# A dilated convolution on one core: the 16-channel scratch laid out by channel, its first chunk transposed by TensorE, a smaller clear, and new queue orders

## The chip, the cores and the metric

The kernel runs on one core of a Trainium2 chip. Its engines are TensorE (PE, with its weight loads PEld), VectorE (DVE), ScalarE (ACT), GpSimd (POOL) and SyncE (SP), which here only issues DMAs. Each engine works through its own list of instructions in order. The metric is the device time of one execution in microseconds (us); lower is better.

## The reference

x has 2 sequences of 16000 steps of 144 channels, all in bf16. A causal convolution with 15 taps, two steps apart, gives 288 channels; half of them go through tanh, half through a sigmoid, the product is multiplied by w_o.

```python
B, T, D, K = (2, 16000, 144, 15)
def reference(x, w, w_o):
    dil = 2
    pad = (K - 1) * dil
    xp = jnp.pad(x, ((0, 0), (pad, 0), (0, 0)))
    h = jnp.einsum('btc,cd->btd', xp[:, pad:pad + T, :], w[0])
    for i in range(1, K):
        off = pad - i * dil
        h = h + jnp.einsum('btc,cd->btd', xp[:, off:off + T, :], w[i])
    f = h[..., :D].copy()
    g = h[..., D:].copy()
    z = jnp.tanh(f) * _sigmoid(g)
    return z @ w_o
```

## The kernel before

The 32000 steps are cut into 128 runs of 250, one for each partition, so that step t of all runs is one tile of 128 x 144. The 250 tiles make two single tiles and 31 octets of eight; the octets after the first (octet 0) are worked in 15 pairs, m = 0 to 14, with two units each (r = 0, 1), 30 units in all. A unit gives eight output tiles.

Of the 144 channels, 128 (called A) need a transposed tile (channels on partitions) for each step, kept in XA. The other 16 (called B) of eight taps are packed on 128 partitions, in XB. The convolution is done with fewer products than taps by a scheme of differences: V, DU and DD hold differences of XA tiles, GX, GU, GV and GD differences of these between octets, and WS, WC, WD, WV and WT sums of weights. DVE makes them; PE multiplies them into PSUM banks (PS), and parts shared by several tiles (UX, UC, UD, UE) are added by DVE and POOL in float32. UE lies in the memory of Xp. ACT takes sigmoid and tanh from PSUM to TG, DVE multiplies the halves into Z (the gate), a DMA transposes Z to ZT, PE multiplies by WOR (w_o laid out for blocks of 128 columns), ACT copies to OS, and SP stores.

How data get to XA and XB after the prologue (stages `load_xchunk`, `load_xa`, `compact_chunk`, `load_xb`, lines 650 to 719):

- A chunk is 16 tiles, two octets. `load_xchunk` loads it to Xr (two buffers).
- `load_xa(o)`: ACT or DVE copies the A channels of octet o to STA (two buffers), SP issues a DMA transpose to XA (lines 678 to 683).
- `compact_chunk(ci)`: the B channels of the chunk go to C16 as 4 groups of 6 rows: two tiles copied (DVE or ACT, line 864) and four differences (POOL, line 668). SP issues a DMA transpose from C16 to T16 (line 669) and a store of T16 to the scratch S16 in DRAM (line 670). In S16 the order is group, row, channel, then 128 partitions.
- `load_xb(o)`: SP shifts part of the previous octet's XB by 32 partitions (XB<-XB) and loads the rest from S16 (line 695). Each load brings one or two groups, 16 channels by 6 or 12 rows of 256 B. For octet 1 and octet 2 the loads are split further, because the halo comes from XBh.

The prologue (0 to some 25 us) loads x to Xp and the weights in five pieces; PE transposes Xp tiles for XA, and the B channels of the prologue go through XBc (in the memory of XS) to XBh with 12 more PE transposes (`b_halo`, line 628). Before these, POOL clears two rows of XBc (line 615) and copies 32 elements (line 622). POOL also clears all of Z (line 546) and WOR (line 547), and issues the 16 loads of w_o to WOR (line 1200). Two matmuls against the identity (line 1126) open banks 6 and 7.

The order of every engine's work is written out by hand: `_Graph` numbers operations as they are added, and TABLE gives for each engine the list of these numbers in the order of issue; `place` follows it. ON_ACT lists the copies (`free_copy`) that ACT makes instead of DVE. Waits between engines are worked out from what each operation reads and writes, so an operation waits only for its own inputs, buffers and banks, but everything behind it on its engine waits with it. The constants DMA_LAT, FIRST, SEM_LAT, MM and each operation's `dur` are a planner's estimates; they choose which PSUM banks are used, and the order in which an operation's waits stand, and no instruction's length.

Of the kernel before, what the change touches and what calls it, by code (L numbers as in the profile page):

```python
# [12 lines left out]
DMA_LAT = 2.8  # L13
DMA_RATE = 280e3
FIRST = (1.12, 1.1)
# [1360 lines left out]
```

## Time and profile before

| | us |
|---|---|
| median of 3 runs | 312.39 |
| lowest, highest | 311.79, 314.02 |
| the profiled execution | 311.91 |
| its span, first to last instruction | 310.2 |

The profiled execution is 0.48 us under the median. The page gives busy time by engine and a picture of the span in 40 slices, each digit the busy share in tenths (9 is 90% or more):

```profile
PE   8998779999999999999999999999999999999995
DVE  2999799999997999999999999989989897998755
ACT  2698578788888899899988988999889999888885
POOL 3495440444331333433234443213343331233330
DMA  7937789597999798895749999699757569431543
```

PE is full but for the slices from 23 to 47 us and the last one. In every timeline row the columns are start, length, engine, line, instruction, output and inputs, count, and in brackets how long the engine stood before it and what released it. In the rows of groups (`| busy, mean ns | idle`), busy time is in us and the mean of one in ns.

### The profile page before, as it was taken

What the parts mean: (1) busy time and instruction counts of PE and PEld (TensorE: products, weight loads), DVE (VectorE), ACT (ScalarE), POOL (GpSimd) and SP (SyncE); (2) the same over time, 40 slices, a digit from 0 to 9 for tenths busy, and PEclk for the clock granted to TensorE, in tenths of its full rate; (3) what the DMA queues carried; (4) which work ended last, traced back from release to release, by engine and by line L of the source; (5) the groups of instructions that cost most, each with busy time, mean ns of one, the idle gap of its engine ahead of it and who ended that gap; (6) DMA issues with size and microseconds to landing.
All of it is one profiled execution on the core that took longest, in us unless ns stands there. A gap on an engine that the chain in (4) does not pass through costs nothing.

```text
span 310.2 us, 7389 instructions
## 1 busy us (share of the span) xinstructions
PE 299.9 (97%) x2553; PEld 234.1 (75%) x2553; DVE 279.5 (90%) x607; ACT 264.0 (85%) x786; POOL 110.4 (36%) x105
## 2 busy tenths in 40 slices
PE   8998779999999999999999999999999999999995
PEld 7876556777767788787778777777878777777874
DVE  2999799999997999999999999989989897998755
ACT  2698578788888899899988988999889999888885
POOL 3495440444331333433234443213343331233330
PEclk9999999999999999999999999999999999999999
DMA  7937789597999798895749999699757569431543
GB/s 212 300 61 183 174 206 225 132 244 176 190 201 220 137 279 192 193 211 130 196 128 200 230 229 233 99 204 244 164 143 151 163 152 182 125 90 50 142 100 130
DMA packets 107631, 54.48 MB, mean 176 GB/s; under 512 B 95549, under 2 KB 98445, under 8 KB 107595
## 3 DMA queue, kind: packets, MB, share of 16 engines
q1 hardware_dynamic: 107049, 53.63, 76.5%
q0 software_dynamic: 512, 0.33, 0.5%
q8 instruction: 20, 0.33, 0.5%
q14 instruction: 16, 0.13, 0.1%
q10 hardware_dynamic: 34, 0.05, 0.1%
HBM read 15.93 MB, written 10.69 MB: 86 GB/s over the span
## 4 chain that ended last, share of the span: by engine, by line
PE 83%; DMA 8%; DVE 5%; issue 1%; SPq 1%; ACT 1%; DVEq 0%
PE PS L811 72%; PE PS L921 8%; DMA XA<-STA 4%; DMA ZT<-Z 2%; PE PS L564 1%; DMA XB<-s 1%; DVE PS L1065 1%; DVE Xp L991 1%; PE PS L592 1%; DVE V L723 1%; DVE STA L864 1%; DVE DD L723 0%; SPq L695 0%; SPq L669 0%; DVE Z L838 0%
## 5 line engine op out<-in xcount | busy, mean ns | idle before, releaser
L1001 POOL TENSOR_TENSOR UX<-UC,XS 128x576 f32<-128x576 f32 x60 | 83.7, 1413 | 177.2 <-ACT UC L450 117.3
L811 PE MATMUL PS<-WB,XB 128*128 128x288 bf16 x360 | 101.8, 286 | 0.0
L964 ACT ACTIVATE PS<-PS 128x288 f32<-128x288 f32 x213 | 81.9, 418 | 7.8 <-PE PS L811 6.4
L811 PE MATMUL PS<-WA,GD 128*128 128x288 bf16 x450 | 88.0, 286 | 0.4 <-DVE PS L1065 0.2
L450 ACT ACTIVATE TG<-PS 128x288 bf16<-128x288 f32 x180 | 65.1, 418 | 6.8 <-PE PS L811 5.7
L864 ACT ACTIVATE OS<-PS 128x432 bf16<-128x432 f32 (+1 forms) x93 | 42.8, 493 | 16.5 <-PE PS L921 15.6
L1065 DVE TENSOR_TENSOR PS<-PS,Xp 128x288 f32<-128x288 f32 x120 | 50.1, 460 | 3.1 <-ACT OS L864 1.0
L811 PEld LDWEIGHTS PS<-WA,GD 128*128 128x128 bf16 x450 | 40.6, 98 | 15.7 <-DVE PS L1065 2.3
L991 DVE TENSOR_TENSOR Xp<-PS,UD 128x576 f32<-128x576 f32 x60 | 43.2, 753 | 10.3 <-PE PS L811 6.9
L1065 DVE TENSOR_TENSOR PS<-PS,UX 128x288 f32<-128x288 f32 x120 | 50.1, 459 | 0.7 <-POOL UX L1001 0.3
L811 PE MATMUL PS<-WS,GU 128*128 128x288 bf16 x210 | 44.8, 286 | 1.8 <-DMA XB<-s 1.8
L921 PE MATMUL PS<-WOR,ZT 128*128 128x144 bf16 (+1 forms) x322 | 40.8, 253 | 1.1 <-DMA ZT<-Z 1.1
L811 PEld LDWEIGHTS PS<-WB,XB 128*128 128x128 bf16 x360 | 35.2, 98 | 8.7
L811 PE MATMUL PS<-WC,GV 128*128 128x288 bf16 x210 | 37.9, 286 | 0.0
L811 PE MATMUL PS<-WD,DD 128*128 128x288 bf16 x210 | 34.0, 286 | 0.0
L921 PEld LDWEIGHTS PS<-WOR,ZT 128*128 128x128 bf16 x322 | 27.5, 98 | 7.3 <-DMA ZT<-Z 1.4
L453 ACT ACTIVATE TG<-PS 128x144 bf16<-128x144 f32 x140 | 29.8, 301 | 2.5 <-PE PS L811 1.9
L838 DVE TENSOR_TENSOR Z<-TG 128x576 bf16<-128x576 bf16 (+1 forms) x63 | 27.7, 442 | 3.9 <-ACT TG L450 3.3
L811 PEld LDWEIGHTS PS<-WS,GU 128*128 128x128 bf16 x210 | 19.9, 98 | 7.5 <-DVE GD L800 2.1
L811 PE MATMUL PS<-WC,GX 128*128 128x288 bf16 x120 | 23.5, 286 | 1.8 <-DVE Xp L991 1.8
L723 DVE TENSOR_TENSOR V<-XA 128x1024 bf16<-128x1024 bf16 (+2 forms) x38 | 23.6, 623 | 1.1 <-DMA XA<-STA 0.9
L811 PE MATMUL PS<-WT,DU 128*128 128x288 bf16 x120 | 24.5, 286 | 0.1
(98 smaller groups left out, 435.8 us busy)
## 6 DMA issues: line engine op xcount, KB each, us to landing
Xr<-in_x_dram SPq DMA_DIRECT2D x15, 648.0 KB, 5.1
out_dram<-OS SPq DMA_DIRECT2D x30, 288.0 KB, 3.1
XB<-XB SPq DMA_DIRECT2D x29, 288.0 KB, 3.4
XB<-s SPq DMA_DIRECT2D x60, 48.0 KB, 3.0
s<-T SPq DMA_DIRECT2D x15, 96.0 KB, 3.5
WA<-in_w_dram SPq DMA_DIRECT2D x2, 288.0 KB, 4.5
ZT<-Z SPq DMA_TRANSPOSE x32, 3.5
Xp<-in_x_dram SPq DMA_DIRECT2D x2, 252.0 KB, 4.4
```

The source lines that it names most:

```text
L450: return e.activation(bass.AP(t[:].tensor, off + (0 if st > 0 else n), [[row, NP], [st, 2], [1, n]]), bass.AP(PS[:].tensor, lo * 512 + c0, ...
L453: ins = e.activation(bass.AP(t[:].tensor, off + i * n, [[row, NP], [1, n]]), bass.AP(PS[:].tensor, q.phys * 512 + c0, [[8 * 512, NP], [1, ...
L564: g.add("pe", [lambda t: t.matmul(PS[:, BANK_O * 512:BANK_O * 512 + 128], lhsT=HEAT[:], rhs=HEAT[:], start=True, stop=True)] * n, r=["HEAT ...
L723: return g.add("dve", lambda v: v.tensor_tensor(dst(), a(), b(), ALU.subtract), r=r, w=wk, dur=dur, prio=2, lock=True)
L811: return lambda t: t.matmul(bank(b), lhsT=lhs(), rhs=rhs(), start=start, stop=True, skip_group_check=True)
L838: g.add("dve", lambda v: v.tensor_tensor(dst(), TG[:, s, 1, 2 * k:2 * k + n, :], TG[:, s, 0, 2 * k:2 * k + n, :], ALU.mult), r=[("TG", s, ...
L864: return (lambda e: e.activation(dst(), src(), ACT.Copy)) if eng == "act" else (lambda e: e.tensor_copy(dst(), src()))
L921: return t.matmul(PS[:, c0:c0 + n * D], lhsT=ZT[:, zt, blk_, :], rhs=WOR[:, wi_:wi_ + n, :].rearrange("p a b -> p (a b)"), start=first, st ...
L964: g.add("act", lambda e: e.activation(bank(c), bank(b), ACT.Copy), r=[("bank", b)], w=[("bank", c)], dur=0.29, prio=prio)
L991: return v.tensor_tensor(ue(u % NU, q, 0, 2).rearrange("p (v n) -> p v n", v=2), src, UD[:, u % NUD, :, :], ALU.add)
L1001: op = g.add("pool", lambda p: p.tensor_tensor(UX[:, u % NU, h, :, :], UC[:, 0, :, :], bass.AP(XS[:].tensor, h * N2, [[2 * N2, NP], [0, 2] ...
L1065: g.add("dve", lambda e, dst=dst, src=src, ua=ua: e.tensor_tensor(bank(dst), bank(src), ua(), ALU.add), r=[("bank", src), ("UX", us, h) if ...
```

## The change

Five things are changed together.

1. C16 is laid out channel, group, row instead of group, row, channel. Its copy and its subtraction now write two or four neighbouring elements at a time and read Xr at a step of one tile (288 B). S16 follows: a channel's 24 rows of a chunk lie together, and a load of one or two groups takes one run of 6 or 12 rows for each channel (1.5 or 3 KB), or two runs where the two groups lie in different chunks.
2. For chunk 0 alone, the DMA transpose is replaced by three PE transposes into bank 7 and one ACT copy to T16. The two matmuls of line 1126 are added after it.
3. POOL clears only columns 720 to 863 of the one Z buffer that octet -1 uses.
4. TABLE and ON_ACT are new. There is one operation more, so numbers from 117 on are one higher. ON_ACT has 14 copies instead of 11 (10 of C16 and 4 of STA, before 8 and 3).
5. The planner's constants and a few `dur` are changed.

```diff
-DMA_LAT = 2.8
+DMA_LAT = 3.2
-FIRST = (1.12, 1.1)
+FIRST = (1.12, 1.5)
...
-        C16 = sb("C16", [NP, NX, 4, 6 * DB], BF16)
+        C16 = sb("C16", [NP, NX, DB, 4, 6], BF16)
...
-        g.add("pool", lambda p: p.memset(Z[:], 0.0), w=[("Z", i) for i in range(NZ)], dur=1.2)
+        g.add("pool", lambda p: p.memset(Z[:, -1 % NZ, 5 * D:6 * D], 0.0), w=[("Z", -1 % NZ)], dur=0.25)
...
             def xr(t, n=4):
-                return bass.AP(Xr[:].tensor, (s * XCH + t) * D + DA, [[NX * XCH * D, NP], [4 * D, 4], [D, n], [1, DB]])
-            cc = C16[:, s, :, :].rearrange("p a (t c) -> p a t c", c=DB)
+                return bass.AP(Xr[:].tensor, (s * XCH + t) * D + DA, [[NX * XCH * D, NP], [1, DB], [4 * D, 4], [D, n]])
+            cc = C16[:, s, :, :, :]
...
+            if ci:
+                g.add("sp", lambda e: e.dma_start_transpose(T16[:, s, :, :], C16[:, s, :, :, :].rearrange("p a b c -> p (a b c)")), r=[("C16", s, 0), ("C16", s, 1)], w=[("T16", s)], dur=1.3, dma="xb", nbytes=3 * 32768)
+            else:
+                tb = HB[7]
+                g.add("pe", [lambda t, i=i: t.transpose(PSb[:, tb.phys * 1024 + 128 * i:tb.phys * 1024 + 128 * i + 128],
+                                                        C16[:, s, :, :, :].rearrange("p a b c -> p (a b c)")[:, 128 * i:128 * i + 128], ID[:]) for i in range(3)],
+                      r=[("C16", s, 0), ("C16", s, 1), "ID"], w=[("bank", tb)], dur=0.23)
+                g.add("act", lambda e: e.activation(T16[:, s, :, :].rearrange("p a b -> p (a b)"), PSb[:, tb.phys * 1024:tb.phys * 1024 + 384], ACT.Copy),
+                      r=[("bank", tb)], w=[("T16", s)], dur=0.42)
...
             def s16(q, n):
-                return bass.AP(S16, q * 6 * DB * 128, [[128, DB], [DB * 128, 6 * n], [1, 128]])
+                c, b = q // 4, q % 4
+                if b + n <= 4:
+                    return bass.AP(S16, (c * 384 + 6 * b) * 128, [[24 * 128, DB], [1, GR * n]])
+                return bass.AP(S16, (c * 384 + 6 * b) * 128, [[24 * 128, DB], [(384 - 18) * 128, 2], [1, GR]])
```

The lists of TABLE are too long to show. Read with the renumbering undone, they say, for the stretch that is spoken of below:

- SP: the first 17 issues are the same. Then, before: DMA transpose of chunk 0, XA for octets 1 and 2, an XB copy, the S16 store of chunk 0, two XB copies and a third, the DMA transpose of chunk 1, six XB loads, ZT, the Xr load of chunk 2, the S16 store of chunk 1, XA for octets 3 and 4. After: XA for octet 1, the S16 store of chunk 0, XA for octet 2, the Xr load of chunk 2, two XB copies, the DMA transpose of chunk 1, eight XB issues (octet 1 is whole with the fifth, octet 2 with the eighth), ZT, the S16 store of chunk 1, XA for octets 3 and 4.
- POOL: before: the clears of XBc, the copy of 32 elements, two WOR issues, the clear of Z, the C16 subtraction. After: the clears of XBc, two WOR issues, the copy, three WOR issues, the C16 subtraction; the clear of Z stands ten places further on, after the tenth WOR issue.
- ACT: the XBh copies stand as eight tiles, the scaling of WB, four tiles, then two STA copies, the C16 copy, an STA copy, the new copy to T16, and an STA copy. The C16 copy of chunk 1 stands four places further on.
- PE: the halo transposes of eight tiles come before those of four; the three new transposes stand at place 35. No operation of PE is moved by more than 19 places in the whole list of 977.
- DVE: the sum WT of the first two entries is made at place 36 instead of 45; after the first addition to UE, one STA copy and the C16 copy of chunk 2 leave the stretch up to the third such addition, and one DD enters it.

More of the change, by code (lines that the diff above doesn't have):

```diff
@@ L20 @@
 TABLE = {
[73 rows of a table removed]
[73 rows of a table added]
 }
-ON_ACT = (112, 217, 429, 589, 748, 1064, 1226, 1385, 1551, 1703, 2029)
+ON_ACT = (110, 218, 275, 428, 430, 588, 908, 1067, 1227, 1393, 1702, 1704, 2023, 2182)
 class _Op:
@@ L545, in _conv_wavenet_kernel @@
         g.add("pool", lambda p: p.memset(XBc[:, 0:2, MB - 1, :], 0.0), w=["XBcz"], dur=0.2)
-        g.add("pool", lambda p: p.memset(Z[:], 0.0), w=[("Z", i) for i in range(NZ)], dur=1.2)
-        g.add("pool", lambda p: p.memset(WOR[:], 0.0), w=["WORz"], dur=1.9)
+        g.add("pool", lambda p: p.memset(Z[:, -1 % NZ, 5 * D:6 * D], 0.0), w=[("Z", -1 % NZ)], dur=0.25)
+        g.add("pool", lambda p: p.memset(WOR[:], 0.0), w=["WORz"], dur=2.0)
         first("sp", ld_wb(0), [("WB", 0)], 0.5, "wb", 73728)
@@ L615, in zf @@
                     return p.memset(XBc[b_ * SEG:b_ * SEG + 1, :, MB - H // 4 - 1:MB, :], 0.0)
-                g.add("pool", zf, r=hk, w=hk + ["XBcz"], dur=0.35)
+                g.add("pool", zf, r=hk, w=hk + ["XBcz"], dur=0.55)
             def fix(p):
@@ L622, in fix @@
                 return p.tensor_copy(dst, s)
-            g.add("pool", fix, r=xp_keys[3], w=hk, dur=0.3)
+            g.add("pool", fix, r=xp_keys[3], w=hk, dur=0.6)
             for o, tiles, bb in ((-1, range(E0 - 4, E0), 7), (0, range(E0, E0 + 8), 6)):
@@ L657, in _conv_wavenet_kernel @@
         NGR = 2 * (NOCT - 1)
-        S16 = nc.dram_tensor("s16", (NGR * 6, DB, 128), BF16).ap().tensor
+        S16 = nc.dram_tensor("s16", (NGR * 6 * DB, 128), BF16).ap().tensor
         def compact_chunk(ci):
@@ L664, in xr @@
             def xr(t, n=4):
-                return bass.AP(Xr[:].tensor, (s * XCH + t) * D + DA, [[NX * XCH * D, NP], [4 * D, 4], [D, n], [1, DB]])
-            cc = C16[:, s, :, :].rearrange("p a (t c) -> p a t c", c=DB)
-            free_copy(lambda: cc[:, :, 0:2, :], lambda: xr(2, 2), [("Xr", s)], [("C16", s, 0)], 0.13, 0.27)
-            g.add("pool", lambda p: p.tensor_tensor(cc[:, :, 2:6, :], xr(2), xr(0), ALU.subtract), r=[("Xr", s)], w=[("C16", s, 1)], dur=0.6, lock=True)
-            g.add("sp", lambda e: e.dma_start_transpose(T16[:, s, :, :], C16[:, s, :, :].rearrange("p a b -> p (a b)")), r=[("C16", s, 0), ("C16", s, 1)], w=[("T16", s)], dur=1.3, dma="xb", nbytes=3 * 32768)
+                return bass.AP(Xr[:].tensor, (s * XCH + t) * D + DA, [[NX * XCH * D, NP], [1, DB], [4 * D, 4], [D, n]])
+            cc = C16[:, s, :, :, :]
+            free_copy(lambda: cc[:, :, :, 0:2], lambda: xr(2, 2), [("Xr", s)], [("C16", s, 0)], 0.2, 0.31)
+            g.add("pool", lambda p: p.tensor_tensor(cc[:, :, :, 2:6], xr(2), xr(0), ALU.subtract), r=[("Xr", s)], w=[("C16", s, 1)], dur=0.7, lock=True)
+            if ci:
[7 more added lines that the diff above has]
+                      r=[("bank", tb)], w=[("T16", s)], dur=0.42)
             g.add("sp", lambda e: e.dma_start(bass.AP(S16, ci * 384 * 128, [[128, NP], [128 * 128, 3], [1, 128]]), T16[:, s, :, :]), r=[("T16", s)], w=[("S16", ci)], dur=0.5, dma="xb", nbytes=3 * 32768)
@@ L695, in xdma @@
                 g.add("sp", lambda e: e.dma_start(out(), in_()), r=r, w=w, dur=0.5, dma="xb", nbytes=n)
-            def rows(p0, n, slot, g0, ng):
-                return bass.AP(XB[:].tensor, p0 * ROW + (slot * 2 + g0) * GR, [[ROW, n], [128, 6 * ng], [1, 128]])
             def flatr(p0, n, slot, g0, ng):
@@ L703, in s16, with rows @@
             def s16(q, n):
-                return bass.AP(S16, q * 6 * DB * 128, [[128, DB], [DB * 128, 6 * n], [1, 128]])
+                c, b = q // 4, q % 4
+                if b + n <= 4:
+                    return bass.AP(S16, (c * 384 + 6 * b) * 128, [[24 * 128, DB], [1, GR * n]])
+                return bass.AP(S16, (c * 384 + 6 * b) * 128, [[24 * 128, DB], [(384 - 18) * 128, 2], [1, GR]])
+            def rows(p0, n, slot, g0, ng, q):
+                if q % 4 + ng <= 4:
+                    return flatr(p0, n, slot, g0, ng)
+                return bass.AP(XB[:].tensor, p0 * ROW + (slot * 2 + g0) * GR, [[ROW, n], [GR, 2], [1, GR]])
             q0 = 2 * (o - 1)
@@ L710, in load_xb @@
                 xdma(lambda: flatr(48, DB, s, 0, 1), lambda: flatr(0, DB, bslot(0), 1, 1), xbk(0), [("XB", s, 0, 1)], DB * GR * 2)
-                xdma(lambda: rows(48, DB, s, 1, 1), lambda: s16(0, 1), [("S16", 0)], [("XB", s, 0, 2)], DB * GR * 2)
-                xdma(lambda: rows(32, DB, s, 0, 2), lambda: s16(0, 2), [("S16", 0)], [("XB", s, 0)], DB * GR * 4)
-            xdma(lambda: rows(0, DB, s, 0, 2), lambda: s16(q0, 2), [("S16", ci)], [("XB", s, 2)], DB * GR * 4)
+                xdma(lambda: rows(48, DB, s, 1, 1, 0), lambda: s16(0, 1), [("S16", 0)], [("XB", s, 0, 2)], DB * GR * 2)
+                xdma(lambda: rows(32, DB, s, 0, 2, 0), lambda: s16(0, 2), [("S16", 0)], [("XB", s, 0)], DB * GR * 4)
+            xdma(lambda: rows(0, DB, s, 0, 2, q0), lambda: s16(q0, 2), [("S16", ci)], [("XB", s, 2)], DB * GR * 4)
             if o > 1:
-                xdma(lambda: rows(16, DB, s, 0, 2), lambda: s16(q0 - 1, 2), [("S16", chunk_of(8 * o - 8)), ("S16", ci)], [("XB", s, 1)], DB * GR * 4)
+                xdma(lambda: rows(16, DB, s, 0, 2, q0 - 1), lambda: s16(q0 - 1, 2), [("S16", chunk_of(8 * o - 8)), ("S16", ci)], [("XB", s, 1)], DB * GR * 4)
             else:
                 xdma(lambda: flatr(16, DB, s, 0, 1), lambda: flatr(0, DB, bslot(0), 1, 1), xbk(0), [("XB", s, 1, 0)], DB * GR * 2)
-                xdma(lambda: rows(16, DB, s, 1, 1), lambda: s16(0, 1), [("S16", 0)], [("XB", s, 1)], DB * GR * 2)
+                xdma(lambda: rows(16, DB, s, 1, 1, 0), lambda: s16(0, 1), [("S16", 0)], [("XB", s, 1)], DB * GR * 2)
         TR = 128
@@ L1124, in _conv_wavenet_kernel @@
                 direct(k, HB[n], pi, t0, t1)
-        for b in range(6, 8):
-            g.add("pe", [lambda t, b_=HB[b]: t.matmul(bank(b_), lhsT=ID[:], rhs=WB[:, 0, :], start=True, stop=True, skip_group_check=True)],
-                  r=["ID", ("WB", 0)], w=[("bank", HB[b])], dur=MM)
         for n, k in enumerate(KS):
@@ L1133, in _conv_wavenet_kernel @@
         compact_chunk(0)
+        for b in range(6, 8):
+            g.add("pe", [lambda t, b_=HB[b]: t.matmul(bank(b_), lhsT=ID[:], rhs=WB[:, 0, :], start=True, stop=True, skip_group_check=True)],
+                  r=["ID", ("WB", 0)], w=[("bank", HB[b])], dur=MM)
         load_xb(1)
```

146 rows, old and new, of the table TABLE are left out of this document.

## The prediction

> **What bounds the kernel now.** I read the page's busy shares first, then the list of what TensorE (PE) waited for, then the table of windows, and last the timeline of each engine from 8 to 50 us. Of the windows, the columns are PE, weight loads, DVE, ACT and POOL, then clock, DMA share and GB/s.
>
> ```profile
> span 310.2 us, 7389 instructions
> PE 299.9 (97%) x2553; PEld 234.1 (75%) x2553; DVE 279.5 (90%) x607; ACT 264.0 (85%) x786; POOL 110.4 (36%) x105
> PE PS L811 <- DMA XB<-s: 1.8, 1, 1.8
> PE PS L811 <- DVE Xp L991: 1.8, 1, 1.8
> PE PS L921 <- DMA ZT<-Z: 1.1, 1, 1.1
> ...
> PE PS L811 <- DVE WT L646: 0.6, 1, 0.6
> 40.00:50.00 10.00, 8.09 (x66) 5.45 (x65) 9.93 (x18) 6.83 (x20) 3.19 (x2) 1.00 0.88 209
> 50.00:60.00 10.00, 10.00 (x83) 7.14 (x81) 9.94 (x23) 8.41 (x24) 3.40 (x3) 1.00 0.78 169
> 60.00:100.00 40.00, 38.74 (x325) 29.59 (x322) 37.74 (x81) 34.95 (x109) 13.03 (x11) 1.00 0.97 203
> 100.00:200.00 100.00, 100.00 (x852) 79.26 (x851) 96.20 (x206) 91.96 (x286) 34.56 (x29) 1.00 0.84 189
> 200.00:280.00 80.00, 79.79 (x677) 62.41 (x675) 73.57 (x158) 72.11 (x224) 25.93 (x20) 1.00 0.74 161
> ```
>
> PE is busy 97% of the span, at full clock, and from 100 to 200 us it has no gap, so no reordering there can gain. The change removes no matmul. What can be won are the four waits listed: 1.8 (XB at 31 us), 1.8 (DVE at 45), 1.1 (ZT at 92) and 0.6 (WT at 24): 5.3 us together, the ceiling. DVE is the next engine: 9.93 and 9.94 of 10 us busy from 40 to 60.
>
> **Where the first wait comes from.** In the timeline (start, length, engine, line) the chain that ends in it reads:
>
> ```profile
> 13.06 0.60 POOL L622 COPY XS<-Xp 128x32 bf16<-128x32 bf16 x1
> 13.61 1.24 POOL L1200 DMA_DIRECT2D WOR<-in_w_o_dram  x2
> 14.85 3.00 POOL L546 MEMSET Z<- 128x3456 bf16 x1
> 17.79 1.08 POOL L668 TENSOR_TENSOR C<-Xr 128x256 bf16<-128x256 bf16 x1
> 18.90 1.29 SPq L669 DMA_TRANSPOSE T<-C  x1
> 20.23 2.67 SPq L683 DMA_TRANSPOSE XA<-STA  x2
> 23.71 0.58 SPq L670 DMA_DIRECT2D s<-T  x1
> 26.29 1.35 SPq L669 DMA_TRANSPOSE T<-C  x1
> 27.68 3.73 SPq L695 DMA_DIRECT2D XB<-s  x6
> 32.66 0.28 PE L811 MATMUL PS<-WS,GU 128*128 128x288 bf16 x1 [1.83 <-DMA XB<-s]
> 33.59 0.76 DVE L991 TENSOR_TENSOR Xp<-PS,UD 128x576 f32<-128x576 f32 x1 [1.67 <-PE PS L811]
> ```
>
> The 3.00 us memset of Z holds POOL before the subtraction into C16; the DMA transpose of C16 goes out only at 18.90, the store to S16 at 23.71, the six XB loads from 27.68, and PE stands 1.83. DVE, done with its list 1.67 us earlier, stands with it.
>
> **The change part by part.**
>
> *Z and the DMA transpose of chunk 0.* The memset shrinks from 3456 columns to 144 and stands after ten of the sixteen WOR issues; 3.00 us leave POOL ahead of the subtraction, three more WOR issues (0.62 each by 13.61) come ahead of it, so C16 is whole about 1 us earlier. The DMA transpose (1.29 on SP, and 23.71 - 18.90 = 4.8 until the store goes out) becomes three PE transposes and one ACT copy.
>
> ```profile
> 11.90 1.09 POOL L615 MEMSET XS<- 1x512 bf16 x2 [8.26 <-ACT XS L558]
> 14.20 0.67 PE PS L628 x12
> 14.46 1.51 ACT L631 ACTIVATE UX<-PS 128x512 bf16<-128x512 bf16 x2 [0.67 <-PE PS L628]
> 16.06 2.18 ACT L678 ACTIVATE STA<-Xr 128x512 bf16<-128x512 bf16 x4
> ```
>
> Three transposes at 0.67 / 12 cost PE 0.17 us, all of it on the bound. The copy, by 1.51 us for twelve tiles, is 0.38 on ACT.
>
> *The new PE wait.* PE is in order, so what stands behind the three transposes waits for C16. From 14.04, where PE reaches the halo transposes, the new list has 12 transposes (0.67) and 27 matmuls (0.12 each by 83 in 10 us) ahead: 17.95. ACT has, from the end of eight halo transposes at 14.5: XBh of eight tiles 1.0, WB 0.55, XBh of four 0.5, two STA copies 1.09, C16 0.55 (0.55 is 2.18 / 4): 18.2. POOL is done near 17.5. So PE waits 0.25; with a subtraction of twice 1.08 it is 0.6, with ACT ahead 0. I take 0.25.
>
> *The halo copy moved behind two WOR issues.* On POOL the copy at 13.06 now stands behind 1.24 us of issues. One ACT copy ahead of the memsets at 11.90 is moved earlier, worth about 0.2, so the copy ends near 14.6 instead of 13.66, and PE, there at 14.04, waits 0.5 (0 to 0.8; no cover: PE's next entries stand behind it).
>
> *SP's queue.* New order: the transpose of XA for octet 1, the S16 store, XA for octet 2, the next Xr load, two XB copies, the DMA transpose of chunk 1, then eight XB issues. XA goes out at 18.1 (STA copied by then), the store at 19.4 instead of 23.71, XA at 20, Xr and two copies to 23, the transpose (it waits for an ACT copy that now stands behind the first TG) to 25, then 8 x 0.62 (3.73 / 6) = 5 to 30. Octet 1 is whole with the fifth of them: 25 + 3.1 + 3.0 to land = 31.1, when PE gets there. Octet 2 is whole with the eighth, near 33, and PE asks for it 0.7 us after octet 1, so it waits up to 1.1, and nothing if the issues take 0.58, as the store to S16 did, and land a little sooner. I keep 0.4 of the wait: 1.43 gained (0.7 to 1.83). The Xr load passed in front lengthens this by one issue; XA for octets 3 and 4 move up with the rest.
>
> *WT.* Its sum stands at place 36 of DVE's list instead of 45: the 0.6 goes, 0.59 gained.
>
> *S16 by channel.* A channel's six rows lie together, so an XB load has 16 runs of 3 KB (or 32 of 1.5) instead of 192 of 256 B.
>
> ```profile
> out_dram<-OS SPq DMA_DIRECT2D x30, 288.0 KB, 3.1
> XB<-XB SPq DMA_DIRECT2D x29, 288.0 KB, 3.4
> XB<-s SPq DMA_DIRECT2D x60, 48.0 KB, 3.0
> L668 POOL TENSOR_TENSOR C<-Xr 128x256 bf16<-128x256 bf16 x15 | 10.6, 710 | 5.0 <-DMA Xr<-in_x_dram 5.0
> L864 DVE COPY C<-Xr 128x128 bf16<-128x128 bf16 x7 | 1.4, 201 | 0.0
> ```
>
> Six times the bytes land in 3.4 us where these take 3.0, so landing is mostly fixed; I take no gain (0 to 1 us each), since from 100 us on PE waits for no load. The price is the reading of C16's sources at a step of 288 B: 0.71 us each on POOL, fifteen times; it stays off the path while DVE has room (third rival). I take no cost.
>
> **The wait that is late next.** The second wait hangs on DVE:
>
> ```profile
> 39.12 0.69 DVE L723 TENSOR_TENSOR V<-XA 128x1024 bf16<-128x1024 bf16 x1 [0.36 <-DMA XA<-STA]
> 42.32 3.26 POOL L1001 TENSOR_TENSOR UX<-UC,XS 128x576 f32<-128x576 f32 x2 [3.99 <-ACT UC L450]
> 42.43 1.90 DVE L723 TENSOR_TENSOR DD<-V 128x1024 bf16<-128x1024 bf16 x1
> 44.25 1.62 DVE L864 COPY STA<-Xr 128x1024 bf16<-128x1024 bf16 x1
> 45.79 0.74 DVE L991 TENSOR_TENSOR Xp<-PS,UD 128x576 f32<-128x576 f32 x1
> 46.59 0.42 PE L811 MATMUL PS<-WC,GX 128*128 128x288 bf16 x2 [1.83 <-DVE Xp L991]
> L723 DVE TENSOR_TENSOR DD<-V 128x1024 bf16<-128x1024 bf16 x33 | 24.4, 750 | 0.0
> L864 DVE COPY STA<-Xr 128x1024 bf16<-128x1024 bf16 x23 | 11.3, 495 | 0.0
> ```
>
> PE's gain by 33 us is 1.43 + 0.59 - 0.17 - 0.25 - 0.5 = 1.10, and DVE's addition of 33.59 moves up as much (its room is 1.67). Between it and the one at 45.79 the new DVE list loses an STA copy (0.50) and the C16 copy (0.20, now ACT's), gains a DD (0.75), and the 0.36 wait for XA goes: 0.31. So PE resumes 1.41 earlier there. DD and STA took 1.90 and 1.62 beside POOL's two UX where their means are 0.75 and 0.50, 2.3 us lost. If the new order meets POOL less, up to 2.3 more comes free, of which PE can use 1.83 + 1.10 - 1.41 = 1.5; if as much, 0. I take 0.3, near the lower end, since both sides move up together.
> [...]
>
> *ZT at 92 us and the rest.* Beside the C16 copy above, two STA copies more sit on ACT before 90 us and two C16 copies fewer: 1.0 - 0.4 = 0.6 us off DVE. Of the 1.1 I take that, 0.6. ON_ACT puts three more copies on ACT in all, which has 8 us of idle time in 100 to 200. The order of the tail is the same but for neighbours: 0.
>
> **The sum.** 1.10 + 0.31 + 0.3 + 0.6 = 2.31 us off the profiled execution of 311.91 us (span 310.2 and 1.7 around it): 309.6. The median of the runs, 312.39, is 0.5 above that execution, so against it the gain is 0.9%.
>
> **The rivals.**
> First, *all waits go*: no halo wait, no wait for C16, no meeting with POOL, ZT in time: 5.3 - 0.17 = 5.1, 306.8; with one of them left 307.5. For it: each wait is single. Against it: DVE is 99% busy to 60 us.
> Second, *DVE holds the gain*: the second wait grows by what the first gives back, since the DVE work up to 60 us is the same but for 0.3 us; PE gains little but 0.6 (WT) and half of XB, less the new waits of 0.9: about 0.6, 311.3. Against it: DVE stood 1.67 us for PE.
> Third, on the other side, *the strided subtraction*: if POOL reads 288 B apart so slowly that DVE's steps with two SBUF inputs are held. DVE's idle time from 60 to 280 us is 2.26 + 3.80 + 6.43 = 12.5 us, over some 12.4 chunks (fifteen in 267 us) 1.0 each. Below 1.7 us per subtraction it costs nothing; at four times 0.71 it costs (2.13 - 1.0) x 12.4 = 14 us: 323.6. For it: nothing in the trace reads so far apart on POOL in volume. Against it: the halo copy of 16-element runs is 0.60 for 32 elements, so much of 0.71 is fixed.
> [...]
>
> **How the numbers follow.** About 1% is what a measurement of this kernel can tell from no change: 3.1 us, so faster means below 309.3 and slower above 315.5. Forecast (308.3 to 310.6): 0.45. All waits go (306.6 to 308.3): 0.20. DVE holds (310.6 to 312.8): 0.25. The strided subtraction decides: 0.06, and new waits of the order (PE's 0.8 + 0.8 with nothing won, 313.5): 0.04. The range 306.7 to 312.8 leaves out the last two. Faster: 0.20 and 0.21 of the forecast, 0.41. Slower: 0.06 and 0.01. The rest, 0.52, is the same.
>
> **What would show it.** Right: the first XB wait below 0.5, WT's gone, a PE wait near 18 us for C16 and one near 14 for XS, the S16 store near 19.4, DVE's second Xp near 44. Wrong: L668 over 1.7 us; the XB wait standing; gaps on PE after 100 us that the trace before does not have.

## The result, and the profile after

| | before | after |
|---|---|---|
| median of the runs taken side by side, us | 312.23 | 309.09 |
| lowest, highest | | 308.58, 309.64 |
| the profiled execution | 311.91 | 309.4 |
| its span | 310.2 | 307.6 |

The ratio is 0.9896 with a 95% interval of 0.9859 to 0.9932: about 1% faster. Not all of it need be waits: of 87 executions of the kernel before that were taken beside the experiments below, 53 had a mean granted clock of TensorE of 0.995 or less (median 312.96 us) and 34 one of 0.998 or more (311.18), while the six of the changed kernel were all at 0.999 or more; the two profiled executions (0.999 and 1.0) hold nothing of this. The changed kernel has 13 lines more ahead of most of what was spoken of: PE's line 811 is 824, its 921 is 934, DVE's 991 is 1004, the copies of 864 are 877, the store of 670 is 678, the transposes of XA are 691 and the XB loads 703. The subtraction (668) and the clear (546) keep their numbers; the new PE transposes are line 673 and ACT's copy to T16 is line 676.

The page's totals and the list of what PE waited for (us in total, times, longest), after:

```profile
span 307.6 us, 7370 instructions
PE 300.8 (98%) x2556; PEld 233.9 (76%) x2556; DVE 279.9 (91%) x604; ACT 266.4 (87%) x774; POOL 111.4 (36%) x105
PE PS L564 <- DVE HEAT L495: 1.1, 1, 1.1
PE PS L824 <- ACT PS L977: 0.8, 1, 0.8
PE PS L824 <- DVE XA L606: 0.7, 1, 0.7
PE PS L824 <- DVE WT L646: 0.4, 1, 0.4
PE PS L824 <- DVE GU L806: 0.4, 1, 0.4
```

The waits for XB, for DVE's addition at 45 us and for ZT are gone. Small ones for an ACT copy, XA and GU are new, and one of 0.4 for WT stands at another place than the 0.6 before; the one for HEAT stands at the start of both kernels. The table of windows says where PE won (second number: PE busy), first the kernel before, then after:

```profile
0.00:40.00 40.00, 36.48 (x318) 28.91 (x319) 31.40 (x77) 26.19 (x59) 21.96 (x35) 1.00 0.74 189
40.00:60.00 20.00, 18.09 (x146) 12.59 (x145) 19.87 (x40) 15.24 (x43) 6.58 (x5) 1.00 0.83 189
```

```profile
0.00:40.00 40.00, 36.83 (x317) 27.81 (x318) 33.05 (x76) 26.71 (x61) 19.81 (x35) 1.00 0.81 197
40.00:60.00 20.00, 20.00 (x166) 14.78 (x164) 19.07 (x42) 18.42 (x51) 7.78 (x6) 1.00 0.98 203
60.00:100.00 40.00, 39.45 (x332) 29.58 (x331) 38.80 (x84) 35.60 (x103) 14.45 (x12) 1.00 0.86 190
```

Up to 40 us PE gained only 0.35 us, from 40 to 60 it gained 1.91, and from 60 to 100 0.71 (39.45 against 38.74). From 100 to 200 PE is without a gap (100.00 of the 100 us), as before. PE's own busy time grew by 0.9 (299.9 to 300.8), so that 2.6 are left in the span.

The timeline after, with the rows of POOL, PE, SP and DVE that answer to the chain shown of before:

```profile
14.42 0.54 POOL L622 COPY XS<-Xp 128x32 bf16<-128x32 bf16 x1
...
16.55 0.98 POOL L668 TENSOR_TENSOR C<-Xr 128x256 bf16<-128x256 bf16 x1
...
19.01 0.33 PE L673 MATMUL PS<-ID,C 128*128 128x128 bf16 x3
...
19.97 0.57 SPq L678 DMA_DIRECT2D s<-T  x1
...
24.07 0.54 PE L824 MATMUL PS<-WS,DU 128*128 128x288 bf16 x3 [0.77 <-ACT PS L977]
...
31.69 0.42 PE L824 MATMUL PS<-WT,DU 128*128 128x288 bf16 x2 [0.39 <-DVE WT L646]
...
34.29 0.74 DVE L1004 TENSOR_TENSOR Xp<-PS,UD 128x576 f32<-128x576 f32 x1
...
42.61 0.68 DVE L736 TENSOR_TENSOR DD<-V 128x1024 bf16<-128x1024 bf16 x1
42.69 3.36 POOL L1014 TENSOR_TENSOR UX<-UC,XS 128x576 f32<-128x576 f32 x2 [4.46 <-ACT UC L450]
43.63 0.76 DVE L1004 TENSOR_TENSOR Xp<-PS,UD 128x576 f32<-128x576 f32 x1 [0.34 <-PE PS L824]
```

The subtraction starts 1.24 us earlier (17.79 before), the store to S16 3.74 earlier (23.71). DVE's first addition to UE comes 0.70 later (33.59 before) and its third 2.16 earlier (45.79).

### The profile page after: what moved, and what is told of

Its sections match the earlier page's. It is cut to its first block, busy times and chain, and to the rows that moved or that the text cites. A ratio compares the mean times of both kernels' runs of the same rounds, so it can differ in the third digit from the quotient of the medians.

```text
span 307.6 us, 7370 instructions
## 1 busy us (share of the span) xinstructions
PE 300.8 (98%) x2556; PEld 233.9 (76%) x2556; DVE 279.9 (91%) x604; ACT 266.4 (87%) x774; POOL 111.4 (36%) x105
## 2 busy tenths in 40 slices
DMA packets 96719, 54.38 MB, mean 177 GB/s; under 512 B 83421, under 2 KB 86797, under 8 KB 96683
## 4 chain that ended last, share of the span: by engine, by line
PE 83%; DVE 10%; DMA 3%; SPq 1%; issue 1%; ACT 0%; DVEq 0%
PE PS L824 74%; PE PS L934 9%; DMA WA<-in_w_dram 2%; DMA XA<-STA 2%; DVE DD L736 1%; DVE V L736 1%; DVE DU L736 1%; DVE WC L646 1%; SPq L489 1%; DVE Xp L1004 1%; DVE Z L851 1%; DVE PS L1078 1%; DVE GU L806 1%; DVE WT L646 1%; DVE WD L646 0%
## 5 line engine op out<-in xcount | busy, mean ns | idle before, releaser
L450 ACT ACTIVATE TG<-PS 128x288 bf16<-128x288 f32 x204 | 73.0, 415 | 6.4 <-PE PS L824 5.3
L1078 DVE TENSOR_TENSOR PS<-PS,Xp 128x288 f32<-128x288 f32 x120 | 50.8, 459 | 2.2 <-PE PS L824 0.6
L934 PE MATMUL PS<-WOR,ZT 128*128 128x144 bf16 (+1 forms) x322 | 42.0, 254 | 0.0
L824 PE MATMUL PS<-WD,DD 128*128 128x288 bf16 x210 | 34.7, 287 | 0.0
L736 DVE TENSOR_TENSOR V<-XA 128x1024 bf16<-128x1024 bf16 (+2 forms) x38 | 24.8, 655 | 0.1
L824 PEld LDWEIGHTS PS<-WD,DD 128*128 128x128 bf16 x210 | 19.6, 98 | 6.5 <-ACT PS L977 1.0
```

The lines of the kernel that those rows point to most:

```text
L450: return e.activation(bass.AP(t[:].tensor, off + (0 if st > 0 else n), [[row, NP], [st, 2], [1, n]]), bass.AP(PS[:].tensor, lo * 512 + c0, ...
L736: return g.add("dve", lambda v: v.tensor_tensor(dst(), a(), b(), ALU.subtract), r=r, w=wk, dur=dur, prio=2, lock=True)
L824: return lambda t: t.matmul(bank(b), lhsT=lhs(), rhs=rhs(), start=start, stop=True, skip_group_check=True)
L934: return t.matmul(PS[:, c0:c0 + n * D], lhsT=ZT[:, zt, blk_, :], rhs=WOR[:, wi_:wi_ + n, :].rearrange("p a b -> p (a b)"), start=first, st ...
L1078: g.add("dve", lambda e, dst=dst, src=src, ua=ua: e.tensor_tensor(bank(dst), bank(src), ua(), ALU.add), r=[("bank", src), ("UX", us, h) if ...
```

## The experiments

Each kernel below was run beside the kernel before on the same chip, one of four; across chips the ratios are to be compared. In those whose lists were rewritten, line numbers are smaller.

| kernel | clear of Z | C16 transposed by, layout | order | median, us | ratio to before (95%) |
|---|---|---|---|---|---|
| e1_clear | small | DMA, old | old | 309.09 | 0.991 (0.9877 to 0.9943) |
| p_parts | small | PE, new | old | 311.51 | 0.9978 (0.9947 to 1.0009) |
| p_parts_clean | small | PE, new | old | 308.11 | 0.9887 (0.9854 to 0.9919) |
| p_full | full | PE, new | old | 310.47 | 0.9945 (0.9913 to 0.9977) |
| o_order | small | DMA, old | new | 310.5 | 0.9959 (0.9931 to 0.9986) |
| a_old_layout | small | PE, old | new | 309.77 | 0.9935 (0.9901 to 0.9968) |
| a_full_pin | full | PE, new | new | 309.3 | 0.9918 (0.989 to 0.9947) |

Five more change one thing of another kind; they follow below. The theory at the start: the 3.00 us clear ahead of the subtraction made the chain late, and its removal is the whole gain. The rivals: the transposes on TensorE with the order do it, or the layout.

**The small clear alone** (e1_clear), in the kernel before:

```diff
-p.memset(Z[:], 0.0), w=[("Z", i) for i in range(NZ)], dur=1.2
+p.memset(Z[:, -1 % NZ, 5 * D:6 * D], 0.0), w=[("Z", -1 % NZ)], dur=0.25
```

> The kernel before with one edit: POOL clears only the 144 columns of Z that are read, at the old place. Theory A (the gain comes from the start chain: clear of Z, C16, S16, XB): POOL is free 2.8 us earlier, the S16 store moves from 23.7 to near 21, the XB wait of 1.83 falls below 0.5 and the time falls by 1.0 to 1.8 us. Theory B (the gain comes from where the new lists put the work on DVE, PE and SP): the XB wait shrinks too, but the DVE wait at 45 us grows by most of it; time down by 0 to 0.8 us.

Its timeline, and its list of PE's waits:

```profile
15.05 0.24 POOL L546 MEMSET Z<- 128x144 bf16 x1
...
15.23 0.93 POOL L668 TENSOR_TENSOR C<-Xr 128x256 bf16<-128x256 bf16 x1
...
16.54 1.31 SPq L669 DMA_TRANSPOSE T<-C  x1
...
21.42 0.58 SPq L670 DMA_DIRECT2D s<-T  x1
...
25.39 3.97 SPq L695 DMA_DIRECT2D XB<-s  x6
...
32.39 0.76 DVE L991 TENSOR_TENSOR Xp<-PS,UD 128x576 f32<-128x576 f32 x1
...
40.58 0.69 DVE L723 TENSOR_TENSOR DD<-V 128x1024 bf16<-128x1024 bf16 x1
40.89 3.19 POOL L1001 TENSOR_TENSOR UX<-UC,XS 128x576 f32<-128x576 f32 x2 [3.95 <-ACT UC L450]
41.18 1.63 DVE L864 COPY STA<-Xr 128x1024 bf16<-128x1024 bf16 x1
42.74 0.74 DVE L991 TENSOR_TENSOR Xp<-PS,UD 128x576 f32<-128x576 f32 x1
```

```profile
PE PS L921 <- DMA ZT<-Z: 1.4, 1, 1.4
...
PE PS L811 <- DVE WT L646: 0.9, 1, 0.9
PE PS L811 <- DVE Xp L991: 0.2, 1, 0.2
```

One line gives as much as the whole change. Everything from the subtraction to the XB loads is 2.3 to 2.6 us earlier, the wait for XB is gone, and with it the second: DVE, which had stood 1.67 for PE, starts its first addition 1.20 earlier and its third 3.05 earlier. So 1.20 of the 3.05 are the lateness of the first wait, passed on. About as much more (1.21) is one half of the meeting with POOL: DD starts 0.31 ahead of UX here and takes 0.69, where before it started 0.11 behind UX and took 1.90. The other half stays: the STA copy beside UX still takes 1.63.

All seven executions of this kernel had a granted clock of 0.999 or more. Beside them, the kernel before has a median of 312.17 over all 30 executions and of 310.84 over the ten at 0.998 or more, so that 1.7 of the 3.1 us are left where the clock was nearly the same. That choice may also favour executions of before in which the waits were short.

**All parts in the old order** (p_parts). The lists of before with the three transposes, ACT's copy and the old list of ACT's copies; in the changed kernel's numbers, PE's list reads:

```diff
-73 69 115 116 67 86 87 92 170 93 89
+73 69 115 67 86 87 112 116 92 170 93 89
```

> All parts of the change (C16 and S16 by channel, chunk 0 by TensorE, small clear) in the order of the kernel before, with only the new operations put in and the old one taken out, old choice of copies for ACT and old planner constants. Theory A: most of the gain, 2 to 3 us. Theory B: at most 1.2 us, with the DVE wait near 45 us and the ZT wait near 92 us still there.

It was no faster than before. PE stood 1.3 us for ACT's copy, since the opening matmul of bank 7 (116) came right behind the transposes (112), and ACT had 823 instructions, where before had 786: the planner had chosen other PSUM banks.

**The order alone** (o_order): the new lists with the old layout and the DMA transpose, the small clear.

> The new lists, the new choice of copies for ACT and the new constants, with the old layout of C16 and S16 and chunk 0 by the DMA transpose (put on SP behind the first XA, its store behind the next Xr load); the clear is the small one, since the new lists put it too late for the large one. Theory A: the XB wait comes back with more than 1 us, time within 1 us of before. Theory B: 1.5 to 3 us faster than before, with no DVE wait at 45 us and no ZT wait at 92 us.

With 310.5 it lies 1.4 above the small clear alone, taken on the same chip, and the two intervals overlap a little. PE waits 1.6 us for XB: the DMA transpose of chunk 0 goes out at 19.19 behind a transpose of XA, and its store at 23.27. But the profiled execution, at 308.44, is the shortest of its twelve, so this wait alone does not explain the median. That the new order needs C16 transposed on TensorE fits these rows and is not shown.

**The old layout in the changed kernel** (a_old_layout), with TensorE's transposes kept:

```diff
-        C16 = sb("C16", [NP, NX, DB, 4, 6], BF16)
+        C16 = sb("C16", [NP, NX, 4, 6 * DB], BF16)
...
-                return bass.AP(S16, (c * 384 + 6 * b) * 128, [[24 * 128, DB], [1, GR * n]])
+                return bass.AP(S16, q * 6 * DB * 128, [[128, DB], [DB * 128, 6 * n], [1, 128]])
```

> The changed kernel with C16 and S16 in the old layout (group, row, channel), all else as changed. If the layout is worth nothing in time: within 0.5 us of the changed kernel (0.9896 of before), L668 back at 0.71 us, packets back above 107000, XB loads still landing in about 3.0 us. Rival (11000 fewer packets free the DMA engines): slower than the changed kernel by 1 us or more, with PE waiting for XB or ZT.

309.77 has an interval that overlaps the changed kernel's; the layout is worth nothing that these runs tell. XB loads land in 3.1 us with it and in 3.0 without.

**DVE's meeting with POOL** (a_sta_ahead): the STA copy (282) ahead of DVE's third addition to UE (351).

```diff
-375 348 415 376 377 282 293 295
+375 348 415 376 377 293 295
...
-292 331 289 351 366
+292 331 289 282 351 366
```

> The changed kernel with one DVE step moved: the STA copy of octet 6 stands ahead of the third UE addition, as in the kernel before, where it met POOL's second UX. If the second wait of the kernel before was made by that meeting: the copy takes 1 to 1.6 us instead of 0.42, the third UE addition comes 0.9 to 1.6 us later than 43.6 and PE waits 0.3 to 1.2 us there; time up by 0.3 to 1.2 us. Rival (it was only DVE being late): the copy takes 0.42, the addition comes 0.1 to 0.4 later, no PE wait.

A miss: the copy took 0.41 us there and the addition began at 43.54, as in the changed kernel, yet the time is 311.71 (0.9969, 0.9944 to 0.9994). ACT has 864 instructions instead of 774. A moved copy makes the planner choose other banks, so this run measured the banks as well as the move, if not the banks alone.

**The banks** (a_old_consts): the changed kernel with the old constants, which move no entry of any list.

```diff
-DMA_LAT = 3.2
-FIRST = (1.12, 1.5)
+DMA_LAT = 2.8
+FIRST = (1.12, 1.1)
```

> The changed kernel with the old planner constants (DMA_LAT 2.8, FIRST 1.1). No list changes, but the planner's choice of PSUM banks does: ACT gets 59 instructions more, since fewer pairs of banks are neighbours that one instruction can empty. Theory (single evictions cost time: 90 more of them cost 2.6 us in the run with the STA copy moved): 59 more cost 1.7, so 310.8 (310.2 to 311.6), with ACT busier by 2 us or more. Rival (the constants choose banks and no time, and that run was slow from the moved copy): 308.8 to 309.5.

310.84 (0.9969, 0.9948 to 0.999). Groups of ACT's instructions, after and then with the old constants (busy us, mean ns):

```profile
L450 ACT ACTIVATE TG<-PS 128x288 bf16<-128x288 f32 x204 | 73.0, 415 | 6.4 <-PE PS L824 5.3
L453 ACT ACTIVATE TG<-PS 128x144 bf16<-128x144 f32 x92 | 20.2, 302 | 1.9 <-PE PS L824 1.5
```

```profile
PE 302.5 (98%) x2556; PEld 232.2 (75%) x2556; DVE 280.4 (91%) x604; ACT 268.9 (87%) x833; POOL 110.9 (36%) x105
L450 ACT ACTIVATE TG<-PS 128x288 bf16<-128x288 f32 x160 | 57.3, 418 | 5.7 <-PE PS L824 5.0
L453 ACT ACTIVATE TG<-PS 128x144 bf16<-128x144 f32 x180 | 38.6, 312 | 2.5 <-PE PS L824 1.8
```

Where two halves don't lie in neighbouring banks, one instruction of 415 ns becomes two of 302 to 312. 44 pairs were split, ACT is busy 2.5 us longer, and the kernel takes 1.75 us more. The two planner constants, for which the prediction's sum has no term, hold more than half of the gain in this list.

**All parts in the old order, banks kept** (p_parts_clean):

```diff
-73 69 115 67 86 87 112 116 92 170 93 89
+73 69 115 67 86 87 112 92 170 93 116 89
...
-DMA_LAT = 2.8
+DMA_LAT = 2.6
```

> All parts of the change but the order: layout by channel, TensorE's transposes, the small clear, in the old order and with the old list of ACT's copies. Against the earlier run of this kind the opening matmul of bank 7 stands three entries later, so PE does not stand for ACT's copy at once, and the planner's constant is one with which ACT keeps its count of instructions (787, before 786). Theory (only the clear pays, and the earlier run's 311.5 came from its 37 more ACT instructions and the 1.3 us wait): 309.1 (308.6 to 309.9), as with the small clear alone. Rival (the transposes on TensorE or the layout cost time in the old order): 310.5 to 311.5.

308.11, the lowest median of all, with 787 instructions on ACT. Its interval overlaps that of the small clear alone and of the changed kernel, so it is not shown to beat them; that the parts cost time in the old order is refuted.

**The full clear back in the changed kernel** (a_full_pin). The banks are chosen with the clear at its new place, and only then does it move ahead of the subtraction:

```diff
-p.memset(Z[:, -1 % NZ, 5 * D:6 * D], 0.0), w=[("Z", -1 % NZ)], dur=0.25
+p.memset(Z[:], 0.0), w=[("Z", i) for i in range(NZ)], dur=0.25
...
-200 111 198 209 82 202 219 207 203 23 211
+200 23 111 198 209 82 202 219 207 203 211
```

> The changed kernel with one thing put back: POOL clears all of Z (3456 columns) directly ahead of the subtraction into C16 of chunk 0, as before the change. The choice of PSUM banks is kept as in the changed kernel (774 ACT instructions), so that nothing else moves. Theory (the 3.0 us clear ahead of that subtraction is what the change removes, and all it removes): the subtraction starts 2.7 us later, near 19.3, PE stands for C16 at its three transposes for 1.0 to 1.5 us and again for XB near 31, and the time is back at 311.3 to 312.3. Rival (the new order, TensorE's transposes or the layout earn the gain): the time stays at 308.6 to 309.9.

The theory fell here: 309.3, the rival's time. The timeline (the subtraction is line 673, PE's transposes 678, the store 683, the XB loads 708 in this kernel):

```profile
14.85 3.00 POOL L551 MEMSET Z<- 128x3456 bf16 x1
...
17.80 0.88 POOL L673 TENSOR_TENSOR C<-Xr 128x256 bf16<-128x256 bf16 x1
...
18.73 0.34 PE L678 MATMUL PS<-ID,C 128*128 128x128 bf16 x3 [0.50 <-POOL C L673]
...
19.63 0.40 SPq L683 DMA_DIRECT2D s<-T  x1
...
33.89 0.42 PE L829 MATMUL PS<-WS,GU 128*128 128x288 bf16 x2 [0.52 <-DMA XB<-XB]
```

The clear and the subtraction stand at the very times of the kernel before (14.85, 17.8). But from the subtraction to the store it is 1.8 us, where it was 5.9 (17.79 to 23.71) through the DMA transpose in SP's queue. PE pays 0.50 at the transposes and 0.8 for XB in all, and less in other places: 0.2 for XA instead of 0.7, and none of the 0.4 for WT. So the small clear is enough in the old order, and it is not needed in the new one with TensorE's transposes.

**The full clear in the old order** (p_full): p_parts_clean with that one memset, to tell whether TensorE's transposes alone make it harmless.

> The kernel of p_parts_clean (layout, TensorE's transposes, old order) with the whole of Z cleared ahead of the subtraction, and nothing else different. It tells which part of the change makes the full clear harmless in the run a_full_pin, where the time stayed at 309.3. Theory (TensorE's transposes do: from the subtraction to the store to S16 they need some 2 us where the DMA transpose in SP's queue needed 5.9, so the store stands at 22 as without the clear, and only the wait of PE for C16 at the transposes is new, 1.2 us): 309.3 (308.6 to 310.2), no XB wait near 31. Rival (it is SP's new order with the store ahead of the second XA transpose, or the later place of the transposes on PE): 310.8 to 312.3, with PE standing 1.5 us or more between 17 and 33 us.

310.47. The profiled execution is the longest of its twelve (312.9), so its waits are read for their places:

```profile
18.75 0.88 POOL L600 TENSOR_TENSOR C<-Xr 128x256 bf16<-128x256 bf16 x1
...
19.77 0.33 PE L605 MATMUL PS<-ID,C 128*128 128x128 bf16 x3 [1.49 <-POOL C L600]
...
22.35 0.58 SPq L610 DMA_DIRECT2D s<-T  x1
```

The store is in time (22.07 in p_parts_clean) and there is no wait for XB, as the theory had it; but PE stands 1.49 us at the transposes, and by the medians the full clear costs 2.4 here (310.47 against 308.11; by the ratios, 0.0058 of 312, 1.8, with intervals that just overlap). So neither side held whole: TensorE's transposes repair SP's queue, and put PE behind the subtraction. In a_full_pin that wait was 0.50. PE reaches the transposes at the same time in both (18.28 and 18.23), so the difference in this execution is POOL's: its clear ends at 18.8 here and at 17.8 there. Part of that is x, which came late here: PE waits 1.09 for Xp at 10.79, 0.46 in p_parts_clean, where PE is at the transposes at 17.62. How the difference divides when x comes in time was not tried.

**What POOL's time costs** (a_sub_twice): the subtraction made twice, the first time into a spare buffer.

```diff
-g.add("pool", lambda p: p.tensor_tensor(cc[:, :, :, 2:6], xr(2), xr(0), ALU.subtract)
+g.add("pool", [lambda p: p.tensor_tensor(D16[:, s, :, :, :], xr(2), xr(0), ALU.subtract), lambda p: p.tensor_tensor(cc[:, :, :, 2:6], xr(2), xr(0), ALU.subtract)]
```

> The changed kernel with POOL's subtraction into C16 done twice, first to a scratch tile nobody reads: some 0.95 us more on POOL per chunk, 14 us in all. If DVE's room covers it, as the prediction's third rival has it below 1.7 us per subtraction (here 1.9): 0 to 1.5 us slower than the changed kernel. If each one holds DVE for its whole length and DVE is the bound: 5 us or more.

316.19, a ratio of 1.0129 (1.0089 to 1.0169), 7.1 us over the changed kernel. Its totals with the longest wait of PE, and its windows:

```profile
PE 300.7 (96%) x2556; PEld 233.3 (74%) x2556; DVE 288.7 (92%) x604; ACT 266.9 (85%) x774; POOL 126.2 (40%) x120
PE PS L825 <- DVE V L737: 2.7, 2, 2.0
```

```profile
0.00:40.00 40.00, 34.22 (x301) 26.00 (x301) 33.47 (x72) 24.65 (x55) 22.58 (x38) 1.00 0.72 186
...
60.00:100.00 40.00, 36.78 (x309) 27.45 (x307) 39.49 (x78) 33.35 (x98) 16.54 (x14) 1.00 0.82 179
```

POOL is busy 14.8 us more (126.2 against 111.4), DVE, whose list is the same, 8.8 more (288.7 against 279.9), and PE waits for DVE. The loss falls up to 40 us (34.22 of PE busy, 36.83 in the changed kernel) and from 60 to 100 (36.78, 39.45), where DVE is full (29.86 us busy of the 30 from 10 to 40, 39.49 of the 40); another 1.3 falls from 200 to 280. From 100 to 200, with four POOL instructions more (34, 30 in the changed kernel), PE loses nothing: it is busy for all of the 100 us in both.

**Two tries to go below.** a_table_first moves ACT's sigmoid of SCR (18) to the head of its list, so that the table load (1.28 us at 21.89) no longer stands in front of the 0.77 us wait at 24 us:

```diff
-3 4 36 5 33 43
+3 4 5 18 36 33 43
```

> The changed kernel with the idle sigmoid on SCR moved to the head of ACT's list, ahead of its first copy. If the activation table that sigmoid brings also holds the copy: one table load instead of two, none at 21.9 us, PE's wait of 0.77 for an ACT copy at 24 us gone, time down by 0.3 to 0.8 us. Rival: the load moves but the gain is met by the next wait (XB near 33 us or WT at 31 us), time within 0.2 us.

309.12 (0.9893, 0.9852 to 0.9935). That wait is gone, ACT has one table load instead of two, and PE waits for V at 21.62 (0.17), for DD at 24.52 (0.41) and for WT at 31.88 (0.62) instead. f_wt_zt2 starts from e1_clear and aims at the two waits left there; the moves are made after the banks are chosen (engine, operation, behind which):

```diff
+MOVES = (('dve', 150, 153), ('dve', 152, 150), ('pe', 776, 799), ('act', 777, 802))
```

> The kernel before with the small clear, and two moves aimed at the waits that are left in that run: the two sums WT that PE waits 0.9 us for near 25 us stand four places earlier on DVE, and the projection that waits 1.4 us for ZT near 90 us stands 1.3 us of matmuls later on PE, its ACT copy with it. The choice of PSUM banks is kept. Theory (each of the two waits is single and goes): 309.1 - 0.9 - 1.2 = 307.0 (306.6 to 307.8). Rival (as where ACT's table load was moved, other waits take their place): 308.6 to 309.4.

309.41 (0.9912, 0.9883 to 0.994). In the profiled execution the waits for WT and ZT are gone and PE waits 1.98 for DVE's addition to UE at 45.06, 0.2 in e1_clear, because DD (40.90) started behind POOL's UX (40.63) and took 1.90, as in the kernel before. This execution, at 311.9, is the longest of the twelve, and more than the wait is in it (a row of the windows; its clock is the third number from the end):

```profile
46.00:47.00 1.00, 1.00 (x6) 0.61 (x5) 1.00 (x3) 0.00 (x0) 0.00 (x0) 0.50 1.08 259
```

From 45 to 49 us the granted clock was 0.76, 0.50, 0.50 and 0.53 in the four microseconds, which takes some 1.7 us from PE, an estimate. Its mean over the execution is 0.994, which is also that of many executions of the kernel before. Both times came out as the rivals had them, the second at the upper end of its range. That other waits took the place of those removed is shown for a_table_first, each of them for DVE; for f_wt_zt2 the one execution profiled does not stand for the median.

## Why the prediction was right

The time was 309.6 and is 309.09; the profiled execution gained 2.5 us where the sum had 2.31. The sum is right and several of its terms are not. Up to 40 us it had 0.75 too much (1.10 against 0.35) and from 40 to 60 us 1.30 too little (0.61 against 1.91). These two errors nearly cancel, so that the total came out within 0.2 us is in part luck.

*The chain.* That the clear holds POOL and so the store to S16 was right, and so was the earlier subtraction ("about 1 us", 1.24). The store came at 19.97, forecast at 19.4. Of the wait for XB 0.4 was kept; all of it went.

*The new PE waits.* 0.25 for C16 and 0.5 at the halo were charged; PE listed neither. PE arrived at both a microsecond late (15.03 instead of 14.04, 19.01 instead of 17.95), in part through a wait of 0.73 for XA at 10.52 that the sum did not have. Both waits and the absence of one for WT were named as signs of being right, and none of the three came. Nor had the sum the 0.77 at 24.07 for ACT, behind its table load (1.28 us at 21.89). WT's 0.59 was taken whole, and 0.39 came back at 31.69. So the 1.10 forecast up to 33 us is 0.35 up to 40.

*DVE's wait at 45 us* is the largest miss: 0.31 + 0.3 were taken, and PE won 1.91 from 40 to 60. DVE's addition of 33.59 was to move up by PE's 1.10; DVE was busy without a gap from 25 us to it, and it came 0.70 later. That the third came 2.16 earlier even so lies in the stretch between them, 12.20 us before and 9.34 after: 2.86 less, where the sum had 0.61. The term that failed is the STA copy that leaves DVE's list: it was priced at its mean, 0.50, while the row quoted beside it shows that it took 1.62 in that place; DD, at 1.90, took 0.68 after. Both the copy and the stretch were freed there, 1.12 + 1.22 us, the 2.3 of which the sum took 0.3.

The lengthening left this place and not the whole kernel: no DD takes more than 0.69 us in the changed kernel and no STA copy of DVE's more than 0.43, but the longest V, DU and GV take 1.35, 1.09 and 1.36 (0.69, 0.91 and 0.69 before), and DVE is busy 279.9 us after and 279.5 before, with three instructions fewer. That as much comes back elsewhere is no rule of these runs: in e1_clear, with the list of before, DVE is busy 278.4. In these rows the DD that starts ahead of UX is not lengthened (0.08 ahead after, 0.68; 0.31 ahead in e1_clear, 0.69) and the one that starts behind it is (0.11 behind before, 1.90); and a_sub_twice has 8.8 us more of DVE for 14.8 more of POOL.

*ZT*: 0.6 taken, 0.71 measured from 60 to 100 us; in e1_clear, with the old list of ACT's copies, the wait stays at 1.4, and the kernel is as fast with it.

*The layout* was rightly given no gain, and the subtraction no cost that shows. The group of POOL's subtractions by duration (minimum, median, maximum ns), before and then after:

```profile
L668 POOL TENSOR_TENSOR C<-Xr x15: 658/669/1082, 17.8 to 229.1; 128x256 bf16<-128x256 bf16 x15
```

```profile
L668 POOL TENSOR_TENSOR C<-Xr x15: 858/876/1246, 16.6 to 235.9; 128x256 bf16<-128x256 bf16 x15
```

The median rose by 31% (669 to 876). But the third rival's threshold was wrong. It held that the subtraction is free below 1.7 us, by dividing DVE's idle time evenly over the chunks. Doubled, it is some 1.9 (0.88, and 14.8 / 15 = 0.99 more), for which this gives (1.9 - 1.7) x 12.4 = 2.5 us; it cost 7.1; 5.3 of the 6.6 us that PE loses in the windows fall up to 100 us, where DVE has no idle time to hide it.

*What was costed at nothing:* the constants. The description of the kernel before has them choose banks and change no instruction's length, and the sum has no term for them; by the banks they change how many instructions ACT has.

*The chances.* 0.41 for faster by over 1% and 0.52 for within 1%: at 0.9896 the result lies on the bound between the two.

## What to carry to other kernels

Before several parts are changed together, change the smallest one alone: one memset gave what five parts gave within the intervals, and two cures for one wait do not add. Put the profiled execution beside the others of its kernel, in time and granted clock, before its waits are made to explain a median. Where a planner assigns buffers or banks from estimated times, count the instructions of each engine before comparing two orders: 90 more instructions on ACT hid the effect of a moved copy. Price a moved instruction by the row in its place, not by its group's mean, and do not spread idle time evenly over the work that is to hide in it.

## What the runs showed of the hardware

- With C16's sources read at a step of 288 B and C16 written by channel, the medians rose by about the same on all three engines: POOL 669 to 876 ns, ACT 310 to 420, DVE 190 to 259; in a_old_layout they are 672, 310 and 189. The read step and the write order changed together, so the two are not told apart.
- 10,912 DMA packets fewer (107,631 to 96,719), with 16 or 32 long runs for a load in place of 96 or 192 of 256 B, left the median landing of the XB loads at 3.0 us.
- Work added to POOL in a_sub_twice lengthened DVE's unchanged list: 8.8 / 14.8 = 0.6 us of DVE's busy time for each us of subtraction.
- Behind a wait of PE of some 2.0 us the granted clock fell to 0.50 in two profiled executions: in f_wt_zt2 (wait of 1.98 to 45.06 us) and in p_full (wait for ZT of 1.96 to 93.21, clock 0.50 from 94 to 97). Each fall takes some 1.7 us from PE, an estimate from the clock in each microsecond. Behind waits of 1.97 and 1.93 in a_sub_twice and of 1.83 twice in the kernel before it stayed at 1.00, so these runs show no length from which it falls. The 53 executions of before at 0.995 or less are longer by 1.8 us in the median, about one such fall; that falls of this kind make them so is likely and not shown, since none of them was profiled.
